# Sparse attention followed by a feed-forward block: band v of the first batch by one casting load, and the planner's figures anew

## The chip, the core and the metric

The kernel runs on one core of a Trainium2 chip. The metric is the device time in microseconds of one execution; the median of three runs of the kernel before is 298.2 us (298.0 to 298.53). Engines are named as in the profile: PE (matrix products and transposes), PEld (its weight loads), ACT, DVE, POOL and SP. POOL and SP also issue DMA transfers; only POOL's transfers convert fp32 to fp16 on the way in this kernel, and only SP issues transposing transfers. A step in which the text says "lands" is the moment at which a transfer's data is complete.

## What is computed

```python
# q, k, v: (8, 8, 576, 64) fp32; moe_w_in (512, 2048); moe_w_out (2048, 512); s, b: one number each
scores = scale * np.matmul(q, k.transpose(0, 1, 3, 2))
rel = pos[:, None] - pos[None, :]
mask_local = (rel >= 0) & (rel < 32)                                   # heads 0..3
mask_strided = (rel >= 0) & (pos[None, :] % 32 == pos[:, None] % 32)   # heads 4..7
attn = softmax(where(mask, scores, -1e9));  x = attn @ v               # then (4608, 512)
r = np.maximum(x @ w_in, 0.0)
out = (s * (r * r) + b) @ w_out
```

## The kernel before

**Attention.** There are eight batches of eight heads. Two heads make a pair, so a batch has four pairs: m = 0 and 1 are local (each query sees at most 32 keys back), m = 2 and 3 strided. A local pair works on 6 blocks of 96 queries against 128 keys (96 of the block and the 32 before it), a strided pair on 8 classes of 72 positions. `pair_steps` (from L474) writes a pair's work as a list of steps in fixed order: transposes of q and k on PE (L494, L502), their copies out of PSUM into `qD_*` and `kT*` (posted to ACT or DVE), score products (L623) into PSUM groups of 2 local or 3 strided products, one exponential per group on ACT (L641), AV products (L684) against `v_loc` or `v_str`, reciprocals and multiplications into `x_nat`, and transposes of `x_nat` (L731) whose copies give `xT`, the feed-forward input. Later batches do several of these transposes by SP's transposing transfers instead (`k_dma`, `q_dma`, `x_dma`, L546 to L599).

In batch 0 the mask is applied on PE: before each score product, a product of the identity with a tile of 0 and -30000 (`negs`) is written into the same columns (L620), and the score is added to it. In the other batches the exponentials are multiplied by 0 or 1 on DVE (L649).

**Band v.** For local heads `v_loc` holds v in blocks of 96 rows on partitions 32 to 127; partitions 0 to 31 hold the last 32 rows of the block before, which `rows_before` (L435) copies, once for each pair. A column of ones beside v gives the softmax's sums. For batch 0, SP loads heads 0 and 1 in fp32 into a corner of the still empty `w_out_sb` (`stage_v`, L309), POOL casts them (`cast_v`, L421) and copies the rows before. Heads 2 and 3 come by a casting transfer of POOL (L1365), which is issued behind q and k of all heads. Strided v is loaded to `vs` and cast from there to `v_str`.

**Feed-forward.** The tokens come in nine blocks T of 512. FF1 (`ff1`, L983) forms x @ w_in for 16 slices of 128, relu and square follow on ACT and DVE, FF2 (`ff2`, L1238) multiplies by w_out. From T = 2 on FF2, and for the last two blocks FF1 too, use a seven-product scheme of 2 x 2 blocks (`ff2_seven`, L951; `ff1_seven`, L1208). In the last block the last product, P3, is done for two halves t of 128 tokens, each of which is evicted on DVE and stored by itself (`store`, L878).

**Order.** Nothing loops on the chip: at build time a planner (`Plan`, L19) walks a modelled clock and writes one instruction order for each engine. Each PE step has keys that it needs, a cost in ns and keys that it makes; other engines' work is posted with the keys it waits for, a cost for each engine that may do it, and keys that it makes some latency later (`LAT`, L27). `flush` takes, among the posts that are ready, the one with the earliest ready time plus a weight of its kind (`ORDER`, L124). Times at which loads are expected are put in by hand: `AT` (L1371) for the first ones, `landing` (L1309), a ring on which each load adds its cost, for the rest. `due` (L1515) says how far attention should be ahead of the feed-forward steps. If no step is ready, `keep_running` (L1487) writes filler products on a spare PSUM bank (L1502), to keep PE running.

**Queues.** POOL's first transfers are q and k of the local heads, two heads at a time, then strided q and k, band v of heads 2 and 3, and strided v; then, gated by a one-element copy that reads the landed `qs` (L1386), the four quarters of w_in; then batch 1's loads with w_out. The fetches of batch b + 2 (`fetch_qk`, L1319) are held on POOL by one-element copies that read the strided kT transposes of batch b + 1 (L1323). In the plan such a fetch waits until `q` and `k` of batch b are used, by the keys in L1432 to L1437; for late batches the key `("q", ...)` is made by `q_spread` (L585), which spreads the transposed q over `qD` after the `qT` transfer has landed.

## Time and profile before

| | before |
|---|---|
| median of the runs | 298.2 us |
| profiled execution | 298.86 us |
| its span, first to last instruction | 297.1 us |
| PE busy | 290.5 us, 2802 products |
| DVE busy | 235.3 us |
| ACT busy | 194.3 us |
| POOL busy | 93.7 us |
| granted PE clock | 0.999 |
| FF1 products, L983 | 115.5 us |
| filler, L1502, to 20 us | 7.35 us |
| mask products, L620 | 28 |
| last product starts, ends | 293.30, 293.57 us |

The span is the stretch in which the profile sees instructions; the execution's own time is 1.8 us more than it. PE's products are pipelined, so their busy times overlap, and each lasts longer than the distance to the next: what a product costs when the stream is full is the distance between starts. The busy share is given over the whole span; the head, up to some 23 us, is limited otherwise than what follows, so that the windows by stage matter more than the sums.

### The profile page before, as it was taken

To read this page: it belongs to the slowest core of one execution; us is meant where nothing else is said; L and a number is where in the kernel's file an instruction comes from. 1 tells how busy PE (TensorE), PEld (TensorE's weight loads), DVE (VectorE), ACT (ScalarE), POOL (GpSimd) and SP (SyncE) were. 2 spreads that over 40 slices of the span, in tenths; PEclk is the share of its full clock that TensorE was granted. 3 is DMA by queue.
4 is the path that set the end of the run, shared out by engine and by line. 5 is a ranking of instruction groups with operands and counts; after the bars stand their busy time and mean duration, and the time that the engine had idled before them with its cause. 6 is when DMAs were issued, how large, how long until landed. Compare 5 with 4: busy or idle time off the path is not lost.

```text
span 297.1 us, 7092 instructions
## 1 busy us (share of the span) xinstructions
PE 290.5 (98%) x2802; PEld 220.0 (74%) x2802; DVE 235.3 (79%) x501; ACT 194.3 (65%) x336; POOL 93.7 (32%) x140
## 2 busy tenths in 40 slices
PE   8999999999999999999999999999999999999995
PEld 3775656666556568889767776768888989999984
DVE  5857888798966988787877896759898588888963
ACT  3577957898838798647774878469877545675400
POOL 8873624601980296009710394100000000000000
PEclk9999999999999999999999999999999999999999
DMA  8999999997999499989999999999230300110214
GB/s 136 189 206 203 218 180 184 223 171 119 109 195 149 67 132 138 170 173 122 148 136 144 182 170 105 143 140 207 44 97 0 108 29 9 71 38 3 95 48 142
DMA packets 106152, 38.19 MB, mean 129 GB/s; under 512 B 85414, under 2 KB 103974, under 8 KB 106118
## 3 DMA queue, kind: packets, MB, share of 16 engines
q0 software_dynamic: 60848, 18.23, 62.7%
q1 hardware_dynamic: 45270, 19.51, 36.0%
q8 instruction: 22, 0.36, 0.5%
q14 instruction: 12, 0.10, 0.1%
HBM read 36.99 MB, written 10.62 MB: 160 GB/s over the span
## 4 chain that ended last, share of the span: by engine, by line
PE 88%; DMA 6%; ACT 2%; DVE 2%; POOL 1%; issue 1%; ACTq 0%
PE ps_f L983 28%; PE ps_f L951 22%; PE ps_f L1238 8%; DMA v_loc<-in_v_dram 6%; PE ps_s L623 5%; PE ps_f L1208 3%; PE ps_a L684 3%; PE ps_s L1502 2%; PE ps_a L1208 2%; PE ps_s L951 2%; PE ps_t L1208 2%; PE ps_s L1208 2%; PE ps_t L951 1%; PE ps_s L1238 1%; PE ps_t L684 1%; PE ps_t L502 1%
## 5 line engine op out<-in xcount | busy, mean ns | idle before, releaser
L983 PE MATMUL ps_f<-xT,w_in_sb 128*128 128x512 f16 (+4 forms) x568 | 115.5, 331 | 0.3 <-ACT u L1009 0.3
L1009 ACT ACTIVATE u<-ps_f 128x512 f16<-128x512 f32 x104 | 61.0, 594 | 32.5 <-PE ps_f L983 31.8
L983 PEld LDWEIGHTS <-w_in_sb 128*128 128x128 f16 x576 | 57.4, 114 | 23.2 <-issue 0.5
L951 PEld LDWEIGHTS <-gT 128*128 128x128 f16 x608 | 58.4, 98 | 9.2
L951 PE MATMUL ps_f<-w_out_sb,gT 128*128 128x256 f16 x376 | 55.6, 273 | 0.0
L1017 ACT ACTIVATE gT<-u 128x1024 f16<-128x1024 f16 x29 | 30.7, 1057 | 0.8
L1238 PE MATMUL ps_f<-w_out_sb,gT 128*128 128x512 f16 x112 | 30.4, 379 | 0.0
L951 PE MATMUL ps_f<-w_mix,gT 128*128 128x256 f16 x176 | 25.1, 273 | 0.0
L641 ACT ACTIVATE p_str<-ps_s 72x432 f16<-72x432 f32 (+1 forms) x46 | 20.7, 482 | 6.4 <-PE ps_s L623 5.8
L711 DVE TENSOR_TENSOR x_nat<-ps_a,rec 96x384 f16<-96x384 f32 (+2 forms) x46 | 24.1, 523 | 0.6
L641 ACT ACTIVATE p_loc<-ps_s 128x384 f16<-128x384 f32 x46 | 21.4, 494 | 4.8 <-PE ps_s L623 4.3
L1019 DVE TENSOR_TENSOR gT<-u 128x1024 f16<-128x1024 f16 x27 | 18.5, 686 | 5.9 <-ACT u L1009 5.4
L819 DVE TENSOR_TENSOR gT<-gT 128x1024 f16<-128x1024 f16 x34 | 22.4, 678 | 0.6 <-ACT gT L1017 0.4
L382 POOL DMA_DIRECT2D v_loc<-in_v_dram x24 | 17.7, 757 | 8.6 <-DMA w_out_sb<-in_moe_w_out_dram 5.7
L951 PEld LDWEIGHTS <-S 128*128 128x128 f16 x176 | 17.1, 98 | 2.9
L1238 PEld LDWEIGHTS <-gT 128*128 128x128 f16 x128 | 11.4, 98 | 7.8
L387 POOL DMA_DIRECT2D v_str<-in_v_dram x16 | 13.0, 816 | 12.3 <-PE ps_f L983 3.6
L684 PEld LDWEIGHTS <-p_str 72*128 72x128 f16 x256 | 12.8, 98 | 5.1 <-ACT p_str L641 0.4
L1323 POOL COPY gate<-kT 1x1 f16<-1x1 f16 x6 | 1.5, 256 | 45.0 <-DMA kT<-ks 45.0
L951 PE MATMUL ps_f<-w_mix,S 128*128 128x256 f16 x112 | 15.5, 273 | 0.0
L701 DVE RECIPROCAL rec<-ps_a 96x6 f32<-96x6 f32 (+2 forms) x47 | 8.6, 182 | 8.6 <-PE ps_a L684 8.4
L1149 ACT ACTIVATE gT<-u 128x1024 f16<-128x1024 f16 x12 | 12.7, 1058 | 1.7 <-DVE u L1128 1.4
(237 smaller groups left out, 529.7 us busy)
## 6 DMA issues: line engine op xcount, KB each, us to landing
out_dram<-o SPq DMA_DIRECT2D x34, 256.0 KB, 2.9
w_in_sb<-in_moe_w_in_dram POOLq DMA_DIRECT2D x4, 512.0 KB, 9.7
w_out_sb<-in_moe_w_out_dram POOLq DMA_DIRECT2D x4, 512.0 KB, 9.9
qs<-in_q_dram POOLq DMA_DIRECT2D x6, 288.0 KB, 8.4
ks<-in_k_dram POOLq DMA_DIRECT2D x6, 288.0 KB, 9.7
v_loc<-in_v_dram POOLq DMA_DIRECT2D x24, 72.0 KB, 9.6
ql<-in_q_dram POOLq DMA_DIRECT2D x4, 288.0 KB, 9.0
kl<-in_k_dram POOLq DMA_DIRECT2D x16, 72.0 KB, 3.6
```

What stands on the lines that cost most here:

```text
L382: nc.gpsimd.dma_start(out=vl[LPAD:128, h, :, 0:D], in_=v_band(b, h))
L641: nc.scalar.activation(out=st["pw", g][0:nk, 0:2 * n * nq], in_=st["s", g][0:nk, 0:2 * n * nq], func=AF.Exp, scale=scale)
L684: nc.tensor.matmul(out=st["pa", g][:, n % 6, :], lhsT=st["pw", gp_][0:nk, i * nq:i * nq + WIDE], rhs=vt[0:nk, 2 * mm + e, j, :])
L711: nc.vector.tensor_tensor(out=x_at(0, cnt), in0=st["pa", g][0:nq, 0:cnt, 0:D], in1=st["rec", g][0:nq, 0:cnt].to_broadcast([nq, cnt, D]), o ...
L819: {"V": nc.vector, "P": nc.gpsimd}[eng].tensor_tensor(out=at(out), in0=at(x), in1=at(y), op=op)
L951: nc.tensor.matmul(out=gts[name, T, t][:, 0] if halves else gts[name, T][:, t], lhsT=lhs(k, t), rhs=rhs(k), start=fresh and k == 0 and (ha ...
L983: nc.tensor.matmul(out=gts["h", T, ft][:, lo:hi], lhsT=w_in_sb[ft // 4][:, ct].rearrange("p (x l) -> p l x", l=4)[:, ft % 4], rhs=xT[ct][: ...
L1009: nc.scalar.activation(out=u, in_=gts["h", T, ft], func=AF.Relu)
L1017: nc.scalar.activation(out=g, in_=u, func=AF.Square)
L1019: nc.vector.tensor_tensor(out=g, in0=u, in1=u, op=ALU.mult)
L1208: nc.tensor.matmul(out=st[bk][:, 256 * t:256 * t + 256], lhsT=lhs(t, c), rhs=rhs(c), start=fresh and t == c == 0, stop=t == c == 1, skip_g ...
L1238: nc.tensor.matmul(out=gts[id_], lhsT=gts[T][:, ft, ts * 128:(ts + 1) * 128], rhs=w_out_sb[:, ft, cols], start=(ft == 0), stop=(ft == NFT ...
```

## The change

Band v of batch 0 now comes for all four heads by the casting transfer that batch 1 already used (`load_vl`), issued behind the second pair of local keys and ahead of the strided q and k. The stage in `w_out_sb`, its memset, POOL's casts and the separate transfer of heads 2 and 3 are gone; the two row copies may each go to POOL or DVE. The memsets of `v_loc[0]` move ahead of those of `qD`.

The mask products of batch 0 are one for each PSUM group instead of one for each score product: the tile is broadcast over the 2 or 3 places, in a step of its own (`forbid`) ahead of the group's scores, which needs only the mask tile and a free bank.

The second half of the last P3 is done in two halves of 128 columns, each with its own eviction and store.

In the planner: the first landings (`AT`), the cost of later landings, and one more us on every pending load for each SP transfer (`shared`); shorter transfer latencies, by 3 us less where no load is pending; the fetch of a late batch waits in the plan for the `qT` transfer instead of `q_spread`; weights for single pairs of batch 0, an "ahead" for each sixth of the feed-forward's way, and new values for the weights. The last items set order alone and add no instruction.

```diff
-    LAT = {"A": 70.0, "V": 70.0, "P": 70.0, "D": 12000.0, "X": 7000.0, "Y": 12000.0}
+    LAT = {"A": 70.0, "V": 70.0, "P": 70.0, "D": 10000.0, "X": 7000.0, "Y": 10000.0}
...
+        self.ring, self.loads = 0.0, []
+
+    def landing(self, cost, keys, wait=700.0):
+
+        self.ring = max(self.ring, self.t + 2000.0) + cost
+        for k in keys:
+            self.done[k] = self.ring + wait
+        self.loads.append(keys)
+
+    def shared(self, cost=1000.0):
+
+        self.loads = [x for x in self.loads if self.done[x[0]] > self.t + 1000.0]
+        for x in self.loads:
+            for k in x:
+                self.done[k] += cost
+        if self.ring > self.t:
+            self.ring += cost
...
+    def late(self, k):
+
+        if not isinstance(k, tuple):
+            return 0.0
+        at = k[1] if len(k) > 1 and isinstance(k[1], tuple) else k[2:4] if k[0] == "in" else ()
+        if len(at) == 2 and at[0] == 0:
+            own = k[0] + (k[1] if k[0] == "in" else "") + "0" + str(at[1])
+            if own in self.LATER:
+                return self.LATER[own]
+        return 0.0 if k[2:3] == (0,) else self.LATER.get(k[0], 0.0)
...
+            if eng in "DXY":
+                self.shared()
...
-                self.done[k] = end + (6000.0 if soon else p[4] or self.LAT[eng])
+                self.done[k] = end + (6000.0 if soon else p[4] or self.LAT[eng] - (
+                    3000.0 if eng in "DY" and self.ring < self.t else 0.0))
...
+ORDER = {"g": 1500.0, "S": 1500.0, "in": 2500.0, "w_mix": -400.0, "wc": -400.0, "ev": -1500.0,
+         "c21": 2500.0, "c11": 1500.0, "c12": 2500.0, "C22": -1500.0, "fv": 500.0, "Vb": 1500.0,
+         "x": -800.0, "Ub": -800.0, "xc": 0.0, "fe": 500.0, "k": -1500.0, "fu": 1500.0,
+         "Va": -800.0, "p": 1500.0, "c22": 0.0, "Ua": 2500.0, "e": 500.0, "q": 1000.0, "r": 0.0,
+         "u": 0.0, "q01": 0.0, "p00": 1500.0, "x00": 2500.0, "invl01": -1500.0,
+         "invs00": -1500.0, "k01": 0.0, "r02": -400.0, "lead": 0.9, "r00": -800.0, "x01": 1000.0,
+         "invl00": 2500.0, "invs01": -1500.0, "ahead4": -0.05, "q02": -800.0, "ahead3": -0.1,
+         "r03": 1500.0, "q03": 500.0, "p02": 500.0, "k02": 1000.0, "r01": 500.0, "x03": -400.0,
+         "p01": 1000.0, "x02": 500.0, "q00": 500.0, "k03": -400.0, "p03": 1000.0, "ahead2": 0.05,
+         "ahead5": -0.1, "k00": -800.0, "ahead0": -0.05, "ahead1": 0.0, "SLACK": 400.0,
+         "ahead": 0.05}
...
-    vl_stage = w_out_sb.rearrange("p f m -> p (f m)").bitcast(FP32)[:, 0:NL // 2].rearrange(
-        "p (h t d) -> p h t d", h=2, d=D)
...
-    def stage_v(heads):
-        for h in heads:
-            nc.sync.dma_start(out=vl_stage[LPAD:128, h], in_=v_band(0, h))
-
     nc.sync.dma_start(out=ident, in_=h_ident.ap())
...
-    stage_v(range(2))
     nc.sync.dma_start(out=negs, in_=h_neg.ap())
     nc.vector.memset(ones16, 1.0)
+
+    def v_zero(i):
+        nc.vector.memset(v_loc[i][:, :, :, D:D + 1], 1.0)
+        nc.vector.memset(v_loc[i][0:LPAD, :, 0, :], 0.0)
+        nc.vector.memset(v_str[i][:, :, :, D:D + 1], 1.0)
+
+    v_zero(0)
     for i in range(2):
         nc.vector.memset(qD_loc[i], 0.0)
         nc.vector.memset(kT_loc[i][:, 0:LPAD], 0.0)
-    nc.vector.memset(vl_stage[0:LPAD], 0.0)
     for i in range(2):
         nc.vector.memset(qD_str[i], 0.0)
-    for i in range(NV):
-        nc.vector.memset(v_loc[i][:, :, :, D:D + 1], 1.0)
-        nc.vector.memset(v_loc[i][0:LPAD, :, 0, :], 0.0)
-        nc.vector.memset(v_str[i][:, :, :, D:D + 1], 1.0)
+    v_zero(1)
...
+        if b == 0:
+            load_vl(0)
...
-            src = vl_stage if loc else loaded[b, "vs"].rearrange(
-                "p (h t d) -> p h t d", h=4, d=D)
+            src = loaded[b, "vs"].rearrange("p (h t d) -> p h t d", h=4, d=D)
             for h in range(2 * mm, 2 * mm + 2):
-                copy_on(eng, out=dst[b % NV][0:np_, h, :, 0:D], in_=src[:, h])
-        n = nt * D
-        plan.post([key], {"P": 1000.0} if loc else {"P": 1160.0} if b == 0 else {"A": 2 * (170 + 0.83 * n), "V": 540.0}, g,
-                  [("cast", b, mm) if loc else ("in", "vs", b, mm)])
-        if loc:
-            rows_before(b, mm, ("cast", b, mm))
+                copy_on(eng, out=v_str[b % NV][:, h, :, 0:D], in_=src[:, h])
+        n = ST * D
+        plan.post([key], {"P": 1160.0} if b == 0 else {"A": 2 * (170 + 0.83 * n), "V": 540.0}, g,
+                  [("in", "vs", b, mm)])
 
     def rows_before(b, mm, key):
 
         hs = slice(2 * mm, 2 * mm + 2)
         vl = v_loc[b % NV]
-        src = vl_stage[:, :, :, 0:D] if b == 0 and mm == 0 else vl[:, :, :, 0:D]
 
         def g(eng):
-            copy_on(eng, out=vl[0:LPAD, hs, 1:LT, 0:D], in_=src[128 - LPAD:128, hs, 0:LT - 1])
-        plan.post([key], {"P": 800.0} if b == 0 and mm == 0 else {"P": 800.0, "V": 350.0} if b == 0 else {"A": 700.0, "V": 350.0}, g, [("in", "vl", b, mm)])
+            copy_on(eng, out=vl[0:LPAD, hs, 1:LT, 0:D], in_=vl[128 - LPAD:128, hs, 0:LT - 1, 0:D])
+        plan.post([key], {"P": 800.0, "V": 350.0} if b == 0 else {"A": 700.0, "V": 350.0}, g, [("in", "vl", b, mm)])
...
-                if i % per_s == 0:
+                if i % per_s == 0 and b >= PE_MASK:
                     st["s", g] = bank(group)
                 c = i % per_s * 2 * nq
-                if b < PE_MASK:
-
-                    nc.tensor.matmul(
-                        out=st["s", g][0:nk, c:c + 2 * nq], lhsT=ident[0:nk, 0:nk],
-                        rhs=neg_loc if loc else neg_str, start=True, stop=False)
                 nc.tensor.matmul(
                     out=st["s", g][0:nk, c:c + 2 * nq], lhsT=(st["k"][:, i * nq:i * nq + nk] if loc else st["k"][:, i, 0:SQ]),
-                    rhs=st["q"][:, i].rearrange("d e c -> d (e c)"), start=b >= PE_MASK, stop=True)
-
-            s = Step(f, (2 if b < PE_MASK else 1) * (2 * nq / 2.4 + 8), needs=[("q", id_), ("k", id_)],
-                     group=group if i % per_s == 0 else None)
+                    rhs=st["q"][:, i].rearrange("d e c -> d (e c)"), start=b >= PE_MASK, stop=True,
+                    skip_group_check=b < PE_MASK)
+
+            s = Step(f, 2 * nq / 2.4 + 8, needs=[("q", id_), ("k", id_)],
+                     group=group if i % per_s == 0 and b >= PE_MASK else None)
...
+        def forbid(i, group):
+
+            n = min(per_s, nt - i)
+
+            def f():
+                st["s", i // per_s] = bank(group)
+                nc.tensor.matmul(
+                    out=bank(group)[0:nk, 0:2 * n * nq], lhsT=ident[0:nk, 0:nk],
+                    rhs=(neg_loc if loc else neg_str)[:, None, :].to_broadcast([nk, n, 2 * nq]),
+                    start=True, stop=False, skip_group_check=True)
+            return Step(f, 2 * n * nq / 2.4 + 3, needs=[("negs",)], group=group)
+
         gr = None
         for i in range(nt):
             if i % per_s == 0:
                 gr = group_of("s", b, m)
+                if b < PE_MASK:
+                    steps.append(forbid(i, gr))
...
+        def store(i, k, of, plus, ts=slice(0, 2), ms=slice(0, 256)):
...
+            ends = [(t, k, slice(0, 256)) for t in range(2) for k in range(H)]
+            if last and key == "P3":
+                ends = ends[0:H] + [(1, k, slice(128 * c, 128 * c + 128)) for c in range(2)
+                                    for k in range(H)]
+            for t, k, ms in ends:
...
-                        s.keys = [("P3", T, t)]
-                        s.posts = [([("P3", T, t)], {"V": 420.0},
-                                    store(0, 1, "W", val("Ub"), slice(t, t + 1)),
-                                    [Ws[t]])]
+                        s.keys = [("P3", T, t, ms.stop)]
+                        s.posts = [([("P3", T, t, ms.stop)],
+                                    {"V": 480.0 if ms.stop - ms.start == 256 else 280.0},
+                                    store(0, 1, "W", val("Ub"), slice(t, t + 1), ms),
+                                    [Ws[t]] if ms.stop == 256 else [("P3", T)])]
...
-    def landing(cost):
-
-        nonlocal ring
-        ring = max(ring, plan.t + 2000.0) + cost
-
-        return ring + (6000.0 if plan.t > 60000.0 else 600.0)
...
-                arrive(both(name + "l", b), landing(4600))
+                plan.landing(2400, both(name + "l", b))
...
-            arrive(both(name, b), landing(2000 if b > 1 else 1200))
+            plan.landing(1600 if b > 1 else 1200, both(name, b))
...
-        plan.done["raw", "vl", b] = landing(4600)
+        plan.landing(2700, [("raw", "vl", b)])
...
-            arrive(both("vs", b), landing(5000))
+            plan.landing(3300, both("vs", b), 1200)
...
-    nc.gpsimd.dma_start(
-        out=v_loc[0].rearrange("p h t d -> p (h t) d")[LPAD:128, 2 * LT:4 * LT, 0:D],
-        in_=v.rearrange("b h (t p) d -> b p (h t) d", p=LQ)[0, :, 2 * LT:4 * LT])
     early_v(0)
-    plan.free["P"] = 7100.0
-    plan.free["V"] = 6500.0
-    AT = {"ql0": 5200.0, "kl0": 6900.0, "ql1": 7850.0, "kl1": 8700.0, "qs": 10200.0,
-          "ks": 12100.0, "vl0": 7100.0, "vl1": 13450.0, "vs": 15000.0}
+    plan.free["P"] = 8500.0
+    plan.free["V"] = 6000.0
+    AT = {"ql0": 4500.0, "kl0": 5500.0, "ql1": 6300.0, "kl1": 7100.0, "vl": 9400.0, "qs": 10400.0,
+          "ks": 12400.0, "vs": 14900.0}
...
+    plan.done["negs",] = 5000.0
...
-        ring = 13200.0
+        plan.ring = 13700.0
...
-    plan.done["raw", "v", True, 0] = AT["vl0"]
-    cast_v(0, True, 0, ("raw", "v", True, 0))
-    plan.done["raw", "vl", 0] = AT["vl1"]
-    rows_before(0, 1, ("raw", "vl", 0))
+            plan.landing(cost, [("w_in", c) for c in keys])
+
+    plan.done["raw", "vl", 0] = AT["vl"]
+    for mm in range(2):
+        rows_before(0, mm, ("raw", "vl", 0))
...
-                        [("q", (b, mk)) for mk in range(4)] + [("k", (b, mk)) for mk in range(4)] +
+                        [("qT" if b >= (QB_DMA if mk < 2 else QS_DMA) else "q", (b, mk))
+                         for mk in range(4)] + [("k", (b, mk)) for mk in range(4)] +
...
+        pos += order_.get(f"ahead{int(pos / 3)}", 0.0)
...
-        if len(order) == 2 and i1 % 4 == 0 and f1_pos[i1] > (f2[i2 - 1].pos if i2 else 0.0) + 1:
+        if len(order) == 2 and i1 % 4 == 0 and f1_pos[i1] > (f2[i2 - 1].pos if i2 else 0.0) + lead:
```

## The prediction

> **What bounds the kernel now.** I read the page first: busy shares and the slices.
>
> ```profile
> PE 290.5 (98%) x2802; PEld 220.0 (74%) x2802; DVE 235.3 (79%) x501; ACT 194.3 (65%) x336; POOL 93.7 (32%) x140
> ...
> PE   8999999999999999999999999999999999999995
> DMA  8999999997999499989999999999230300110214
> ```
>
> PE is busy throughout, but a busy PE also counts the filler products of L1502 that keep it running while nothing is ready. So next the windows of that line alone, stage by stage (span; PE busy and count; PEld; clock; DMA share; GB/s).
>
> ```profile
> 0.00:5.33 5.33, 4.28 (x10) 1.35 (x10) 1.00 0.64 115
> 5.33:10.00 4.67, 2.52 (x17) 1.23 (x16) 1.00 1.25 191
> 10.00:15.00 5.00, 0.33 (x3) 0.20 (x3) 1.00 1.46 186
> 15.00:20.00 5.00, 0.22 (x1) 0.10 (x1) 1.00 1.24 206
> 20.00:23.05 3.05, 0.00 (x0) 0.00 (x0) 1.00 1.24 208
> ```
>
> Filler ends at about 19 us; the rings run near 200 GB/s from 2.5 us on. Then the chain of waits inside this head (start, us, what):
>
> ```profile
> 1.05 4.34 PE ps_s L1502 x10
> ...
> 6.02 1.22 PE ps_s L1502 x8
> ...
> 7.62 0.70 PE ps_s L1502 x5
> ...
> 13.96 0.47 DVE kTs L404
> ...
> 18.01 0.82 ACT p_str L641 x2
> 18.84 0.82 ACT x_nat L707 x4
> ...
> 23.21 0.86 PE ps_f L983 x4
> ```
>
> Up to 8.7 us the chain is filler, that is, waiting for q and k to land; then copies on DVE and exponentials on ACT; from 23 us PE itself. From there PE's starts follow one another at the stream rate (in the whole chain of waits "23.21 3.67 PE ps_f L983 x17": 0.216 us each for 512 columns). The exceptions are in the late stage, in the timelines of ACT and PE:
>
> ```profile
> 195.39 0.73 ACT L404 COPY v_loc<-v_loc 32x640 f16<-32x640 f16 x1 [2.47 <-DMA v_loc<-in_v_dram]
> 196.66 1.02 PE L983 MATMUL ps_f<-xT,w_in_sb 128*128 128x512 f16 x4 [0.35 <-ACT u L1009]
> 200.61 0.32 PE L623 MATMUL ps_s<-qD_loc,kT_alt 128*128 128x192 f16 x2 [0.42 <-ACT p_loc L641]
> 293.61 0.48 DVE L882 SCALAR_TENSOR_TENSOR o<-ps_f,sb_all,Ub 128x256 f32<-128x256 f32 x1 [0.39 <-PE ps_f L951]
> ```
>
> ACT waits 2.47 us for the last batch's band v, and PE then loses 196.66 - (195.38 + 7 x 0.109) = 0.52 us and, at 200.61, 200.61 - (199.92 + 0.109) = 0.58 us. The last line is the last eviction; the span ends at 297.1, 3.0 us after it. PE's lost time is therefore: the head (start to steady stream, 23.05 us), about 1.5 us near 196, 200 and 239 us, and the tail of 3.5 us. All else is matmul columns, which the change leaves alone.
>
> **What the Trainium skill says.** "DMA: Bandwidth & Descriptors", Queues, rings and completion order: each DMA engine alternates by packets between the queues that have work. The trace agrees: SP's uncast v and POOL's q and k packets are mixed between 2.9 and 4.8 us. The same page, Specifications: runs below 512 B miss line rate. It agrees: batch 1's band v (the form that is now used for batch 0, 128 B written per run) landed 2.56 us after the load ahead of it (42.79, 45.35) for 288 KB, 115 GB/s where the head has 200. "TensorE: Matmul & The Clock Gate", Architectural detail: ACT and DVE run strictly in order; the u eviction held behind the v_loc copy above shows it.
>
> **The change, part by part.**
>
> *Band v.* Gone: two SP loads (144 KB each, fp32, 256 B runs), the 0.70 us DVE memset of the stage, and POOL's two casts and one row copy (8.39 to 10.2, 1.81 us). Added: one POOL issue of 1.22 us (row of batch 1's load) in place of one of 0.95, moved ahead of the qs, ks and vs issues, which start 1.2 us later; they land 5 us and more after issue, so the ring sets them, not the issue. By the ring: without SP's 288 KB (1.44 us at 200 GB/s) the four q/k loads land earlier, the first 4.89 -> about 4.3, the last 8.29 -> 6.9. Band v then takes 2.56: 9.5 us instead of 10.2 (pair 0 ready after the casts) and 13.2 plus 0.72 (pair 1). qs, ks and the half v took 13.22 - 8.29 = 4.93; with the other half (1.28) 6.2, so ks lands at about 13.1, 1.1 later than now (12.01), or 12.4 if the plan's new figure is right; vs about 14.5 (14.62 now). w_in chunk 0 stays at about 17.1: in front of it the ring carries only 144 KB less written. Its POOL gate waits for qs: 10.3 -> about 11.2, still 3 us before the ring would run dry.
>
> *What that does to the head.* Pair 1 (scores 11.26, AV 14.76, now) is done before ks lands, so ACT's p_loc exponentials (12.86 to 14.12) and DVE's qD_str and x_nat work no longer stand before the strided pairs. Now ks is transposed by 13.3 but its copy waits for DVE until 13.96, scores follow at 14.47. After: ks 13.1, transposes, copy of 0.46, scores at about 14.1. Six exponentials at 0.41 to 0.53 from 14.3 end near 17.2 instead of 18.84: 1.6 earlier. The v_str casts (four of 0.61 after vs) end at 17, so they do not undo it. PE: at 17.1, when w_in chunk 0 lands, about 1.1 us of attention is left (now: 1.8, and 0.7 of waiting), then 16 early FF1 products x 0.216 = 3.46 fill the chain of x_nat and xT: steady stream at 17.1 + 3.46 + 1.1 = 21.6 instead of 23.05. I take -1.5; ends: -2.5 (no attention left, earlier landing), +0.4 (ks 1.1 later and the copies behind it in today's order, less 0.7).
>
> *Wide masks.* 28 products become 12, same columns: 16 x 2.5 ns (82.5 against 80 for 192 columns) = 0.04 us. The first group of a pair, 0.165 or 0.19 us, can now run while q and k are being copied; the others stand between scores as before. Worth 0 to 0.7, and inside the -1.5, because PE has waits there anyway. A bank is held longer; two of four (s, f1) still turn.
>
> *Downstream cover.* Every load used after the head has over 3 us to spare: w_in chunk 1 lands 19.64, used 23.05; w_out chunks 2 and 3 land 39.82 and 42.79, used 42.88 and 46.23. Batch 1's band v lands 45.35, used 46.85, covered by 32 FF2 products (6.9 us). So the 1.5 us survives to 50 us.
>
> *Late gates, landings, order weights.* No instruction is added; order changes everywhere. POOL's late fetches are still held by the gate copies, which wait for the kT transposes of the batch before (16.3 us at 167.6), so an earlier place in the plan does not move them by itself. Cost from -1.5 (all late stalls gone) to +3 (below); I take 0.
>
> *Last output.* The last 8 products of 0.109 become 16 of 0.057: +0.04. The last eviction, 0.48 for 256 columns and 0.75 for 512, is by that slope 0.345 for 128: -0.135. The last store carries 64 instead of 128 KB in 512 B runs: 0 to -0.2, taken -0.1. Its issue (0.34) follows the other half's with 0.4 us between. Sum -0.2.
>
> Total: -1.5 - 0.2 = -1.7. The profiled execution took 298.86 with a span of 297.1, so span 295.4 and 297.2 for such an execution; against the median of 298.2: 296.5.
>
> **Rivals.**
>
> *Late landings too early in the plan (slower).* From a fetch the old plan expects band v after 2.0 + 4.6 + 4.6 + 2.0 + 2.0 + 4.6 + 6.0 = 25.8 us; the trace has 24.5 (batch 6: 133.94 to 158.44) and 26.2 (batch 7). The new one: 2.0 + 2.4 + 2.4 + 1.6 + 1.6 + 2.7 + 0.7 = 13.4 plus 1.0 per SP transfer; 7 and 10 lie in those windows: 20.4 and 23.4. So the row copy comes into ACT's or DVE's order 2.4 us earlier against its data for batch 7, 5.4 for batch 6. Today's 2.47 us of waiting costs PE 1.1; 4.9 would cost about 3.5, +2.4; 4.1 at batch 6 about 2.7. One of them: +2.4 to +3, so 298.2 - 1.7 + 3 = 299.5. It decides from about 1.5 us more of waiting behind such a copy. For it: the arithmetic. Against: for batch 5 the new figure, 17.4, is the trace's 17.8, the copy may go to DVE (half the price there), and the fetch's place in the plan also moves. Chance 0.28.
>
> *Given back.* PE comes 1.5 us earlier to a late stage whose loads do not move (DMA is at 9 tenths until slice 28, and the fetches wait for transposes): ACT's wait of 2.47 becomes 4. Only the tail is left: 298.0. For it: the DMA row. Against: SP's transposes wait for PE and DVE work, which moves too. Chance 0.10.
>
> *More.* The head as forecast and the new order takes the late waits away (1.1 at batch 7, 0.4 at 239): 295.0 to 295.4. Chance 0.18.
>
> *The forecast*, 295.8 to 297.3, has the remaining 0.44.
>
> **Numbers.** This kernel's runs lie within 0.2% of one another, so 0.2% (0.6 us) is what can be told from no change. Faster: forecast, more, and 0.02 of the given-back case: 0.64. Same: 0.08. Slower: 0.28. Low end: the better rival with a little over (294.8); high end: the slower rival with 0.3 over (299.8).
>
> **What would show it.** Right: the first transposes before 4.9 us; no CAST on POOL; AV of pair 1 before 12 us; first FF1 product near 17.3 and steady FF1 by 21.9; tail after the last product under 3.4 us. Wrong in the head: ks after 13.5 or filler between 10 and 17 above 1.5 us with steady FF1 at 23. Wrong late: a v_loc copy on ACT or DVE that waits over 4 us for its DMA near 150 to 200 us, with PE gaps after it, or new SP waits ahead of an xT transpose that FF1 needs. The forecast fails mostly if the late order decides instead of the head.

## The result and the profile after

The changed kernel takes 314.79 us (median of four runs, 313.42 to 317.21) against 298.19 (298.0 to 298.53): 1.056 times as long, 95% interval 1.0495 to 1.0633. The prediction was 296.5 with a range of 294.8 to 299.8. It was wrong in sign, and the measured time lies 15 us above the range. Single executions of a kernel are at times some us longer at a lower clock: the medians and ranges below contain them, the intervals of the ratio do not.

The page of the profiled execution (313.42 us, span 311.6), busy shares and slices:

```profile
PE 294.1 (94%) x2798; PEld 220.4 (71%) x2798; DVE 231.7 (74%) x499; ACT 195.4 (63%) x337; POOL 88.7 (28%) x136
...
PE   7899999999999799889799998899999999999992
...
PEclk9999999999999999999979999999999999999999
```

Before, PE's row was all nines between the first slice and the last. Now there are sevens and eights in the first two slices and between slices 14 and 26, that is from some 100 to 200 us, and the granted clock has one slice of 7 tenths.

The windows of the filler line in the head (span; PE busy and count; PEld; clock; DMA share; GB/s). The rings are the queues of the 16 DMA engines:

```profile
0.00:5.33 5.33, 3.70 (x9) 1.19 (x9) 1.00 0.60 85
5.33:10.00 4.67, 1.72 (x9) 0.77 (x10) 1.00 2.34 128
10.00:15.00 5.00, 1.40 (x11) 0.79 (x10) 1.00 1.29 181
15.00:20.00 5.00, 0.81 (x4) 0.39 (x4) 1.00 1.13 169
20.00:25.05 5.05, 0.49 (x2) 0.19 (x2) 1.00 1.24 208
```

From 10 us on there is 2.7 us of filler where there was 0.55, and between 5.33 and 10 us the rings moved 128 GB/s where they moved 191, although their packets are in flight for longer (2.34 against 1.25). Steady FF1 starts at 25.05 instead of 23.05.

The chain of waits (start, us, what), in the head and in the middle:

```profile
5.14 1.19 POOL qs L417 x2
6.33 0.59 POOL ks L417
6.92 8.29 DMA ks<-in_k_dram
25.22 4.53 PE ps_f L1038 x21
...
97.06 7.31 DMA kT<-ks
...
110.74 4.85 DMA kl<-in_k_dram
115.74 11.48 DMA kT_alt<-kl
128.69 7.01 DMA kT<-ks
```

Before, one load stood in this chain behind the head, the band v of the last batch:

```profile
178.55 16.76 DMA v_loc<-in_v_dram
```

The rest from 23 us on was nearly all PE. Now transposing transfers of SP, of 7 to 11 us each, set the pace, and the chain goes in a loop: kT lands at 104.37, only then does POOL's gate copy let the next batch's q and k be fetched, and kT_alt waits for that k. DMA's share of the chain is 23%; it was 6%. The transposing transfers themselves were not short before either: between 85 and 205 us a kT_alt took 8.4 us from issue to landing and an xT 10.4, but no step of the chain waited for them.

Where PE lost its time can be worked out from the starts: the distance to the next start, less what the columns cost in a full stream (0.216 us for 512, counted nothing for filler; a lower clock counts as loss). The columns themselves come to 281.2 us in both kernels.

| us lost by PE | 0 to 30 | 30 to 100 | 100 to 200 | 200 to the last product | after it | span |
|---|---|---|---|---|---|---|
| before | 8.9 | 0.7 | 1.2 | 0.4 | 3.51 | 297.1 |
| after | 10.8 | 0.5 | 11.6 | 2.1 | 4.24 | 311.6 |

So of 14.5 us, 10.4 are lost between 100 and 200 us, 1.9 in the head, and 2.4 at the end. The large gaps of the middle, in PE's timeline:

```profile
106.98 0.35 PE L781 MATMUL ps_t<-ident,x_nat 72*128 72x72 f16 x6 [1.86 <-DVE x_nat L761]
127.27 0.26 PE L658 MATMUL ps_s<-qD_loc,kT_alt 128*128 128x192 f16 x1 [1.02 <-DMA kT_alt<-kl]
135.74 0.57 PE L658 MATMUL ps_s<-qD_str,kT 128*72 128x144 f16 x6 [1.52 <-DMA kT<-ks]
156.02 1.25 PE L1038 MATMUL ps_f<-xT,w_in_sb 128*128 128x512 f16 x4 [2.22 <-ACT u L1064]
```

Two wait for a transposing transfer directly, the others for an instruction of DVE or ACT that itself waited for one (DVE's x_nat 2.9 us for xT). ACT's timeline just before the last one shows the link:

```profile
152.25 1.35 ACT L449 COPY qD_loc<-qTl 64x576 f16<-64x576 f16 x2 [2.70 <-DMA qTl<-ql]
154.00 1.35 ACT L449 COPY qD_loc<-qTl 64x576 f16<-64x576 f16 x2 [0.39 <-DMA qTl<-ql]
155.37 1.09 ACT L1064 ACTIVATE u<-ps_f 128x512 f16<-128x512 f32 x2
```

The copy stands in ACT's order ahead of the relu, and the relu's PSUM bank is what PE waits for. This gap costs more than its own length. In the windows around it (span; PE, PEld, DVE, ACT, POOL busy; clock; DMA share; GB/s) the granted clock is 0.58 for the next 4 us, about 1.7 us more:

```profile
150.00:156.00 6.00, 3.80 (x30) 2.63 (x29) 2.58 (x7) 3.31 (x6) 1.61 (x2) 1.00 2.10 123
156.00:160.00 4.00, 3.98 (x15) 2.08 (x15) 0.83 (x2) 1.68 (x4) 0.00 (x0) 0.58 1.48 182
160.00:164.00 4.00, 4.00 (x30) 2.83 (x29) 2.61 (x5) 3.33 (x8) 0.00 (x0) 0.99 1.82 116
```

Four products of 512 columns that start at 157.28 take until 158.99, 0.43 us each, twice the 0.216 of a full stream; half the clock was granted for 3.41 us, from 156.68 on.

What makes the transposing transfers late shows in the waits of SP's own queue between 85 and 205 us (us in total, times, longest), here those for q and k loads:

```profile
SPq L614 <- DMA ql<-in_q_dram: 14.1, 5, 6.6
...
SPq L595 <- DMA kl<-in_k_dram: 2.4, 4, 1.3
...
SPq L622 <- DMA qs<-in_q_dram: 1.7, 1, 1.7
```

The kernel before has one such line, of 1.4 us (for strided k). SP's timeline in the kernel before:

```profile
111.75 4.56 SPq L761 DMA_TRANSPOSE xT<-x_nat  x2
116.40 0.53 SPq L1253 DMA_DIRECT2D out_dram<-o  x1
117.04 2.67 SPq L574 DMA_TRANSPOSE qTl<-ql  x2
```

and in the changed one:

```profile
109.44 2.53 SPq L614 DMA_TRANSPOSE qTl<-ql  x2
113.47 3.75 SPq L595 DMA_TRANSPOSE kT_alt<-kl  x2
119.05 2.83 SPq L622 DMA_TRANSPOSE qT<-qs  x2
...
123.51 5.08 SPq L811 DMA_TRANSPOSE xT<-x_nat  x2
```

The next batch's q, k and strided q now stand ahead of xT, and SP, which issues in order, waits for their loads with xT behind it. In the longest of these waits, 6.6 us to 109.4, it issues nothing; xT's transfers are issued at 123.5 instead of 111.8. So far this is an observation; the runs below test it.

At the end, the timeline of DVE and PE:

```profile
305.57 0.75 DVE L932 SCALAR_TENSOR_TENSOR o<-ps_f,sb_all,Ua 128x512 f32<-128x512 f32 x1 [2.68 <-DMA out_dram<-o]
...
306.63 0.34 DVE L932 SCALAR_TENSOR_TENSOR o<-ps_f,sb_all,Ub 128x128 f32<-128x128 f32 x1
307.02 0.38 PE L1006 MATMUL ps_f<-w_out_sb,S 128*128 128x128 f16 x4 [1.64 <-DVE o L932]
308.72 0.35 DVE L932 SCALAR_TENSOR_TENSOR o<-ps_f,sb_all,Ub 128x128 f32<-128x128 f32 x1 [1.75 <-DMA out_dram<-o]
```

PE waits for the first quarter's eviction before it goes on with the second in the same PSUM tile, and that eviction is late because DVE has waited 2.68 us for a store two evictions earlier. The last eviction waits for a store again: three store buffers take turns.

### The profile page after: what moved, and what is told of

It is laid out like the page before. It is cut to its first block, busy times and chain, and to the rows that moved or that the text cites. A ratio compares the mean times of both kernels' runs of the same rounds, so it can differ in the third digit from the quotient of the medians.

```text
span 311.6 us, 7070 instructions
## 1 busy us (share of the span) xinstructions
PE 294.1 (94%) x2798; PEld 220.4 (71%) x2798; DVE 231.7 (74%) x499; ACT 195.4 (63%) x337; POOL 88.7 (28%) x136
## 4 chain that ended last, share of the span: by engine, by line
PE 66%; DMA 23%; POOL 3%; SPq 2%; DVE 2%; ACT 2%; issue 2%; DVEq 0%; POOLq 0%
PE ps_f L1038 20%; PE ps_f L1006 17%; DMA kT<-ks 7%; PE ps_f L1293 7%; PE ps_s L658 4%; DMA kT_alt<-kl 4%; DMA qT<-qs 3%; DMA qTl<-ql 3%; PE ps_f L1263 3%; DMA ks<-in_k_dram 3%; DMA out_dram<-o 2%; PE ps_a L1263 2%; PE ps_s L1263 2%; PE ps_s L1006 2%; PE ps_t L1263 2%; DMA kl<-in_k_dram 2%
## 5 line engine op out<-in xcount | busy, mean ns | idle before, releaser
L1038 PE MATMUL ps_f<-xT,w_in_sb 128*128 128x512 f16 (+4 forms) x568 | 118.1, 333 | 3.1 <-ACT u L1064 3.1
L1006 PE MATMUL ps_f<-w_out_sb,gT 128*128 128x256 f16 x376 | 54.2, 274 | 0.1
L1074 DVE TENSOR_TENSOR gT<-u 128x1024 f16<-128x1024 f16 x27 | 18.3, 680 | 15.7 <-ACT u L1064 15.5
L761 DVE TENSOR_TENSOR x_nat<-ps_a,rec 72x384 f16<-72x384 f32 (+2 forms) x46 | 23.9, 520 | 0.5
L677 ACT ACTIVATE p_loc<-ps_s 128x384 f16<-128x384 f32 x46 | 20.8, 491 | 4.9 <-PE ps_s L658 4.7
L1006 PEld LDWEIGHTS <-S 128*128 128x128 f16 x184 | 17.1, 98 | 4.1 <-issue 1.8
L734 PEld LDWEIGHTS <-p_str 72*128 72x128 f16 x256 | 13.5, 98 | 5.0
L432 POOL DMA_DIRECT2D v_str<-in_v_dram x16 | 13.0, 817 | 13.8 <-DVE rec L751 5.2
L751 DVE RECIPROCAL rec<-ps_a 72x6 f32<-72x6 f32 (+2 forms) x46 | 8.4, 182 | 9.1 <-PE ps_a L734 8.8
L869 DVE TENSOR_TENSOR S<-gT 128x1024 f16<-128x1024 f16 x18 | 12.2, 679 | 2.4 <-PE ps_f L1006 2.4
## 6 DMA issues: line engine op xcount, KB each, us to landing
v_loc<-in_v_dram POOLq DMA_DIRECT2D x24, 72.0 KB, 11.6
```

The lines of the kernel that those rows point to most:

```text
L677: nc.scalar.activation(out=st["pw", g][0:nk, 0:2 * n * nq], in_=st["s", g][0:nk, 0:2 * n * nq], func=AF.Exp, scale=scale)
L734: nc.tensor.matmul(out=st["pa", g][:, n % 6, :], lhsT=st["pw", gp_][0:nk, i * nq:i * nq + WIDE], rhs=vt[0:nk, 2 * mm + e, j, :])
L761: nc.vector.tensor_tensor(out=x_at(0, cnt), in0=st["pa", g][0:nq, 0:cnt, 0:D], in1=st["rec", g][0:nq, 0:cnt].to_broadcast([nq, cnt, D]), o ...
L869: {"V": nc.vector, "P": nc.gpsimd}[eng].tensor_tensor(out=at(out), in0=at(x), in1=at(y), op=op)
L1006: nc.tensor.matmul(out=dst[:, ms], lhsT=lhs(k, t), rhs=rhs(k)[:, ms], start=fresh and k == 0 and (halves or t == 0), stop=t == 1 and k == ...
L1038: nc.tensor.matmul(out=gts["h", T, ft][:, lo:hi], lhsT=w_in_sb[ft // 4][:, ct].rearrange("p (x l) -> p l x", l=4)[:, ft % 4], rhs=xT[ct][: ...
```

## The experiments

Each time is a median; "after" is 314.79, and the kernel before gave 298.12 to 298.43 beside them. The planner makes the order anew for each kernel, so most edits change the order too. The tables give the interval of the ratio to the kernel before.

### One part undone

`a_lat`: the old transposing latencies.

```diff
-    LAT = {"A": 70.0, "V": 70.0, "P": 70.0, "D": 10000.0, "X": 7000.0, "Y": 10000.0}
+    LAT = {"A": 70.0, "V": 70.0, "P": 70.0, "D": 12000.0, "X": 7000.0, "Y": 12000.0}
...
-                self.done[k] = end + (6000.0 if soon else p[4] or self.LAT[eng] - (
-                    3000.0 if eng in "DY" and self.ring < self.t else 0.0))
+                self.done[k] = end + (6000.0 if soon else p[4] or self.LAT[eng])
```

> The changed kernel with the old latencies of SP's transposing transfers in the plan (12 us, and no 3 us less when no load is pending). Theory L (the spreads of qT and qTl on DVE and ACT, and the products that read kT, are placed before those transfers land, because the plan now expects them 2 to 5 us earlier): the 10.7 us that DVE and ACT wait for qT and qTl and the 2.5 us that PE waits for kT go to under 2 us each, PE's loss between 100 and 200 us falls from about 10 us to under 3, time 305 to 307. Theory H (the head is 2 to 3.7 us behind the plan and everything that comes by DMA stays late): waits and time within 3 us of the changed kernel, 312 to 316. Theory W (the new weights and ahead values): the same as H.

`a_order`: the old weights (the whole `ORDER` of before, so neither single pairs' weights nor "lead").

```diff
-ORDER = {"g": 1500.0, "S": 1500.0, "in": 2500.0, "w_mix": -400.0, "wc": -400.0, "ev": -1500.0,
+ORDER = {"g": 1500.0, "S": 2500.0, "in": 2500.0, "w_mix": 0.0, "wc": 1000.0, "ev": 1000.0,
...
```

> The changed kernel with the old weights, ahead, slack and lead. Theory W (the new weights put spreads and copies in the wrong place): time 304 to 307, waits for qT and qTl under 2 us. Theories L and H: the order differs, but the waits for transposing transfers stay at 5 us or more in sum and the time stays at 311 to 317.

`a_band`: band v of batch 0 as before, with the old first landings.

```diff
-        if b == 0:
-            load_vl(0)
...
+    stage_v(range(2))
...
-    AT = {"ql0": 4500.0, "kl0": 5500.0, "ql1": 6300.0, "kl1": 7100.0, "vl": 9400.0, "qs": 10400.0,
+    AT = {"ql0": 5200.0, "kl0": 6900.0, "ql1": 7850.0, "kl1": 8700.0, "qs": 10200.0,
```

> The changed kernel with band v of the first batch loaded, cast and placed as before, with the old first landings; masks, last output and the rest of the planner stay new. All theories: ks of batch 0 lands near 12 us again and the steady stream starts 2 us earlier. Theory H: the loss between 100 and 200 us goes too, time 300 to 304. Theories L and W: only the head's 2 us come back, time 311 to 314.

`a_last`: the last product undivided.

```diff
-            if last and key == "P3":
+            if False:
                 ends = ends[0:H] + [(1, k, slice(128 * c, 128 * c + 128)) for c in range(2)
```

> The changed kernel with the last product undivided, as before. In the changed kernel PE waits 1.79 us between the two halves of the last product, because the second half writes the PSUM tile that the first half's eviction reads, and the last eviction waits 1.75 us for an output buffer. Expected: 2.0 to 2.7 us faster than the changed kernel, 312 to 313, tail after the last product back to 3.5 us; if instead only the output buffers hold the tail (three of them, and stores that take 3.9 us here), the gain is under 1 us.

| | us | range | ratio to before | PE lost 100 to 200 us |
|---|---|---|---|---|
| a_lat | 312.84 | 310.54 to 314.83 | 1.0402 to 1.0532 | 9.6 |
| a_order | 317.52 | 315.86 to 319.93 | 1.0600 to 1.0712 | 12.4 |
| a_band | 311.69 | 310.39 to 314.33 | 1.0404 to 1.0526 | 13.9 |
| a_last | 311.69 | 310.12 to 313.5 | 1.0409 to 1.0503 | 9.9 |

None of the four brings back more than about 3 us. The loss in the middle survives each: a_band repairs the head (PE lost 9.1 there), not the middle, so the middle does not follow from the late head alone; the weights are not the cause; the latencies alone are worth 2 us at most, less than the runs differ. What all four still share, besides the wide masks and the gate in the plan, is the landing figures. a_last gained a little more than expected, though the time after the last product, 4.17 us, did not go back to 3.5: undivided too, an eviction of 512 columns waits 2.13 us for a store there.

### One part alone

`b_plan` is the kernel before with the planner of the change (landings, latencies, gate, weights) and no new instruction; `b_band` has the casting load and its first landings alone, `b_masks` the wide masks alone with the order made anew, `b_last` the halved last output alone, whose order is otherwise that of before.

```diff
# b_plan
-    LAT = {"A": 70.0, "V": 70.0, "P": 70.0, "D": 12000.0, "X": 7000.0, "Y": 12000.0}
+    LAT = {"A": 70.0, "V": 70.0, "P": 70.0, "D": 10000.0, "X": 7000.0, "Y": 10000.0}
...
-            arrive(both(name, b), landing(2000 if b > 1 else 1200))
+            plan.landing(1600 if b > 1 else 1200, both(name, b))
...
# b_band
-    stage_v(range(2))
...
+        if b == 0:
+            load_vl(0)
...
# b_masks
+                if b < PE_MASK:
+                    steps.append(forbid(i, gr))
...
# b_last
+            if last and key == "P3":
+                ends = ends[0:H] + [(1, k, slice(128 * c, 128 * c + 128)) for c in range(2)
+                                    for k in range(H)]
```

> The kernel before with the new planner alone (landings, latencies, gate, weights); band v, masks and last output as before. Theory P (the new figures of the planner are what loses): waits of DVE and ACT for qT and qTl of 5 us or more, PE loses 5 us or more between 100 and 200 us, 304 to 310. Theory H (the later head shifts PE against the loads): 297 to 300, no such waits.

> The kernel before with the casting load of band v and its first landings alone; old planner figures, masks and last output. The head loses about 2 us more than before (ks near 15 us instead of 12). Theory P: that is all, 299.5 to 301.5. Theory H: PE loses 5 us or more between 100 and 200 us as well, 305 to 312. Theory R (any other order loses, because the old one happens to put every spread behind its transfer): a loss in the middle of 2 to 8 us, 302 to 310, as in the run with the wide masks alone.

> The kernel before with the wide mask products alone; the planner's figures, the loads and the last output are the old ones, but the order moves everywhere because the steps are others. Theory P and theory H: 297.3 to 299 (the masks are worth 0 to 0.7 us). Theory R: a loss in the middle of 2 to 8 us, 300 to 306.

> The kernel before with the halved last output alone; every other instruction stands where it stood. If the two halves of the product wait for one another through the shared PSUM tile and the last eviction for an output buffer, as in the changed kernel: 0.8 to 2.5 us slower, 299 to 300.7, with a PE gap of 1 us or more inside the last product. By the prediction's sum: 0.2 us faster, 298.0.

| | us | range | ratio to before | where PE lost more than before |
|---|---|---|---|---|
| b_plan | 305.31 | 304.46 to 306.56 | 1.0218 to 1.0283 | 100 to 200 us: 5.4 instead of 1.2 |
| b_band | 303.32 | 302.95 to 304.66 | 1.0148 to 1.0208 | head 11.0 instead of 8.9; 200 to 240 us 3.4 instead of 0.4 |
| b_masks | 304.4 | 301.1 to 308.6 | 1.0092 to 1.0246 | 100 to 200 us: 3.3; after the last product 5.26 instead of 3.51 |
| b_last | 299.87 | 299.54 to 300.2 | 1.0034 to 1.0073 | after the last product 4.44; 0.4 inside it |

Every part is slower by itself. b_band fits none of its expectations, being slower than the load alone was to make it, without the loss in the middle that the others name. In b_last PE's gap is 0.44 us, not 1. b_masks (1.7% by the ratio, some 5 us) shows what the prediction's rival described, in another kernel: in its ACT timeline the row copy of band v comes ahead of its load,

```profile
196.41 0.72 ACT L443 COPY v_loc<-v_loc 32x640 f16<-32x640 f16 x1 [4.29 <-DMA v_loc<-in_v_dram]
```

4.29 us of waiting, and PE loses 3.3 us between 150 and 200 us. But no new landing figure made this: the masks' steps alone reshuffled the order. To separate a part from its new order, the next runs held the order.

### The order held, and all the planner's times undone

`b_masks_same` writes the wide mask in the step of the first score product of its group, which leaves the order of DVE, ACT, POOL and SP as before; `b_band_same` puts the casting load into the old plan, with PE's and ACT's order as before; `j_slack` is the kernel before with one planner figure moved; `a_times` is the changed kernel with all the old times (landings of later loads, nothing per SP transfer, latencies, gate).

```diff
# b_masks_same
+                if b < PE_MASK and i % per_s == 0:
+                    nc.tensor.matmul(
+                        out=st["s", g][0:nk, 0:2 * n * nq], lhsT=ident[0:nk, 0:nk],
+                        rhs=(neg_loc if loc else neg_str)[:, None, :].to_broadcast([nk, n, 2 * nq]),
...
# b_band_same
-    stage_v(range(2))
...
+        if b == 0:
+            load_vl(0)
...
# a_times: the edits of a_lat and a_landing, and
-                        [("qT" if b >= (QB_DMA if mk < 2 else QS_DMA) else "q", (b, mk))
-                         for mk in range(4)] + [("k", (b, mk)) for mk in range(4)] +
+                        [("q", (b, mk)) for mk in range(4)] + [("k", (b, mk)) for mk in range(4)] +
...
# j_slack
-         "u": 0.0, "SLACK": 600.0, "ahead": 0.05}
+         "u": 0.0, "SLACK": 500.0, "ahead": 0.05}
```

> The kernel before with one wide mask product for each group, issued where the group's first narrow one stood: 28 become 12, and the order on DVE, ACT, POOL and SP stays exactly that of before. If the wide products themselves cost something: slower than 298.2 by over 0.6 us. If the 6 us of the run with the masks alone came from the order that moved with them (theory R): 297.9 to 298.4, no DMA waits beyond those of before.

> The kernel before with band v by one casting load behind the second local keys; casts and stage left out, but every post keeps its place and cost in the plan, so PE's and ACT's orders stay exactly those of before. Theory B (the load itself pushes the head back): ks near 15 us, the steady stream 2 us later, and the time 300 to 301; nothing lost between 60 and 190 us beyond before. Theory H (the later head also loses in the middle): 303 or more. If order alone made the loss of the run with the band alone: 298 to 299.

> The kernel before with nothing but the planner's slack changed from 600 to 500 ns, a value that has nothing to do with transfers; POOL's order stays, that of DVE, ACT and SP moves from some 30 us on. Theory R (the old order happens to fit the transfers, nearly any other loses some us in the middle): 300 to 306, DVE or ACT waiting for transfers for 2 us or more beyond before. Theory P (only the new figures lose): 297.6 to 299.

> The changed kernel with all old times in the plan (landings of later loads, latencies, gate); band v, masks, last output and weights new. Theory P in its narrow form (the new times lose): the waits for qT and qTl go under 2 us, 304 to 307. Theory R: no better than by chance, 307 to 316, with other waits in place of those.

| | us | range | ratio to before |
|---|---|---|---|
| b_masks_same | 299.59 | 298.29 to 303.16 | 1.0019 to 1.0053 |
| b_band_same | 303.19 | 302.39 to 304.11 | 1.0097 to 1.0192 |
| j_slack | 299.45 | 298.49 to 304.0 | 1.0017 to 1.0061 |
| a_times | 304.37 | 302.39 to 304.97 | 1.0127 to 1.0222 |

j_slack: this new order costs about 1 us, not 16. With b_masks above it was some 5 (1.2 of it with the masks alone, see below), with b_late7 below 2.4, so that a few us of any difference between two orders can come from the order alone.

b_band_same: with the order of PE and ACT held, the casting load still costs 4.8 us (5.1 in b_band), more than was expected of the load, and not in the middle: PE lost 0.2 between 100 and 200 us. Its windows show the same slow rings as the changed kernel: 89 GB/s to 5.33 us and 132 to 10 us, against 115 and 191. In its profiled execution the granted clock was also 0.82 between 10 and 15 us and 0.84 to 20 us, which is some 1.7 us; in those of b_band and of the changed kernel it stayed at 1.00 there. So what the late head costs is not one number.

b_masks_same: the masks in the old order are no gain. The time is 1.2 us longer, more than the 0.6 named ahead as the sign that the wide products cost something themselves, and here no order moved but PE's. The profiled execution (298.95) does not show a slower PE: the last product starts at 292.39 instead of 293.30. But DVE waits 2.00 us for a store at the end, and the last store is issued behind two others at 294.01 instead of 294.13, so that the span ends at 297.2 as before. What makes the median longer is open.

a_times takes 10.4 us off the changed kernel, and PE lost 0.1 between 100 and 200 us: the loss in the middle goes with the planner's times.

### Which time it is

`a_landing` brings back the old landing figures of later loads and nothing else. `a_wait_qk` and `a_wait_v` keep the changed kernel's ring and only put back the 6 us behind it, for q and k, or for v. `b_late7` is the kernel before, with band v of the last batch expected 3 us later.

```diff
# a_landing
-            self.done[k] = self.ring + wait
+            self.done[k] = self.ring + (6000.0 if self.t > 60000.0 else 600.0)
...
-            if eng in "DXY":
-                self.shared()
...
-                plan.landing(2400, both(name + "l", b))
+                plan.landing(4600, both(name + "l", b))
...
# a_wait_qk
-                plan.landing(2400, both(name + "l", b))
+                plan.landing(2400, both(name + "l", b), 6000.0)
...
# a_wait_v
-        plan.landing(2700, [("raw", "vl", b)])
+        plan.landing(2700, [("raw", "vl", b)], 6000.0 if plan.t > 60000.0 else 700.0)
...
# b_late7
-        plan.done["raw", "vl", b] = landing(4600)
+        plan.done["raw", "vl", b] = landing(4600) + (3000.0 if b == 7 else 0.0)
```

> The changed kernel with the old figures for later landings (4.6 us for a whole q, k or band v, 6 us more on every load after 60 us, nothing added for SP's transfers); the new transposing latencies stay. Theory S (the landing figures put SP's transposing transfers ahead of the loads that they read, and SP, which works in order, stands: 14.1 us for local q in the changed kernel, none in the kernel before): SP's waits for q and k loads are under 1 us together, the gaps of PE between 100 and 200 us fall from 11.6 to under 3 us, and the time is 303 to 307. Theory T (the latencies of the transposing transfers are the cause, and restoring them alone gave only 2 us because the landing figures hid it): 310 to 313, with copies that wait for qT, qTl and kT as before.

> The changed kernel, whose later q and k loads (local and strided) alone are expected 6 us after their place on the ring instead of 0.7; v is as changed. Theory S: SP's order is mended by this alone: 304 to 308, SP's waits for q and k loads under 2 us together. The rival of the prediction (the row copy of band v, planned too early, holds ACT or DVE): no gain, 311 to 316.

> The changed kernel, whose later v loads alone (band v and strided v) are expected 6 us after their place on the ring; q and k are as changed. Theory S: SP still waits over 8 us for local q, and the time stays at 311 to 316. The prediction's rival (the copy of band v): 306 to 310.

> The kernel before, with band v of the last batch alone expected 3 us later; all orders are as before up to some 190 us. If the 2.47 us for which ACT waits on that load costs PE the 1.1 us counted in the prediction: 297.0 to 297.4, with no wait of ACT for v_loc and a gap of PE under 0.3 us there. If the loss only moves to another step (as with every order tried so far): 298.0 to 299.5.

| | us | range | ratio to before | SP waits for q, k loads, 85 to 205 us | PE lost 100 to 200 us |
|---|---|---|---|---|---|
| after | 314.79 | 313.42 to 317.21 | 1.0495 to 1.0633 | 18.2 | 11.6 |
| a_landing | 302.96 | 301.92 to 303.48 | 1.0125 to 1.0189 | 0 | 0.2 |
| a_wait_qk | 307.57 | 305.12 to 309.92 | 1.0236 to 1.0321 | 0 | 0.0 |
| a_wait_v | 319.3 | 316.29 to 320.73 | 1.0636 to 1.0736 | 20.8 | 15.7 |
| b_late7 | 300.69 | 300.09 to 301.91 | 1.0053 to 1.0103 | 0 | 0.1 |

(a_wait_qk's profiled execution, 309.92 us, is the slowest of its four, at half the clock from 15.3 to 29 us; only its middle is read.) Theory S holds: the landing figures alone are worth 11.8 us, the 6 us for q and k alone 7.2, and the loss in the middle is gone with either. Both are more than any new order without these figures cost here (b_masks, some 5). That a_wait_qk stays 4.6 us behind a_landing was not followed up; its other executions had 0.983 to 0.991 of the clock, those of a_landing 0.992 to 0.998. The same 6 us for v alone made the kernel 4.5 us slower, outside both ranges expected; the loss in the middle grew with SP's waits, and why v's later place makes q's worse was not tried. Over all kernels the sign is plain: those with the new figures for q and k have 13.8 to 21.6 us of such waits of SP (a_lat, a_order, a_band, a_last, a_wait_v and b_plan too), those without 0 to 3.2. SP's timeline in a_landing has xT first again, with the loads landed when their turn comes:

```profile
112.34 4.66 SPq L809 DMA_TRANSPOSE xT<-x_nat  x2
117.56 0.33 SPq L1306 DMA_DIRECT2D out_dram<-o  x1
117.99 3.94 SPq L612 DMA_TRANSPOSE qTl<-ql  x2
```

Two things follow from the early figures: SP stands, and the copies of transposed q on ACT and DVE come too early in their own orders. Both go together in these runs, and no run moved one without the other, so that which of the two costs more stays open.

b_late7 did take away the 2.47 us for which ACT waited in the kernel before (PE lost 0.1 between 150 and 200 us, not 1.2), and the loss came back elsewhere, in PE's timeline at

```profile
231.83 0.49 PE L1208 MATMUL ps_s<-qD_loc,ks 128*128 128x256 f16 x3 [1.65 <-DVE qD_loc L1083]
```

so the kernel got 2.4 us slower, more than either expectation.

### The end, and what is left

`b_tail` is b_last, with the same instructions in the same order, but the last eviction writes to the free buffer of Va. `c_best` is the changed kernel without the three costly parts: the edits of a_band, a_landing and a_last together.

```diff
# b_tail
-                o = op.tile([128, 2, 256], FP32, tag="o", name="o")
+                o = (cp if ms.start else op).tile([128, 2, 256], FP32, tag="Va" if ms.start else "o", name="o")
```

> The kernel before with the halved last output, in the same order of instructions as in b_last (299.87), but the very last eviction writes to a buffer that is free (that of Va) instead of the fourth use of three store buffers. If the reuse of the store buffer is most of what the halved output costs, the last eviction no longer waits 1.59 us, the tail after the last product falls from 4.44 to 3.0 to 3.4 us, and the time is 298.2 to 298.7; PE's gap of 0.44 us between the two halves stays. If the gap or the smaller store is the cost: 299.5 and more.

> The changed kernel with three of its parts undone together: band v and its first landings, the landing figures of later loads, and the halved last output. What stays is the wide masks, the new transposing latencies, the gate in the plan and the new order weights. If the parts add up (a_landing 302.96, less 4.8 for the casting load and 1.4 to 1.6 for the last output): 296.5 to 297.5, which would be faster than before. If each new order has its own small losses, as the other variants of the kernel before show: 298.5 to 301.

b_last and b_tail, last eviction on DVE:

```profile
295.14 0.35 DVE L933 SCALAR_TENSOR_TENSOR o<-ps_f,sb_all,Ub 128x128 f32<-128x128 f32 x1 [1.59 <-DMA out_dram<-o]
```

```profile
294.24 0.35 DVE L933 SCALAR_TENSOR_TENSOR o<-ps_f,sb_all,Ub 128x128 f32<-128x128 f32 x1 [0.48 <-PE ps_f L1007]
```

b_tail took 298.92 us (298.29 to 302.31; ratio 0.9998 to 1.0036), with 3.38 us after the last product where b_last has 4.44. The store buffer was most of what the halved output cost in the kernel before; PE's gap of 0.44 us between the quarters stays in both, and the gain that the halves were counted at is not there even so.

c_best took 300.25 us (299.14 to 303.64; 1.0018 to 1.0064). The parts do not add up to a gain, as the second expectation had it: from a_landing to c_best there are 2.7 us, not the 6.2 to 6.4 counted, and in the profiled execution (302.46 us) PE lost 2.1 us between 150 and 200 us and 1.5 after that. No version that was run beats the kernel before. The 16.6 us go down in steps as 11.8 (landing figures) + 2.7 (casting load and halved output) + 1.8 (masks, latencies, gate and weights, with their order); the rest, 0.2 before rounding, is what the kernel before differed between the two sets of runs. Another order of undoing would give other steps: a_band and a_last, undone first, are 3.1 us each. The gate alone was not run.

## Why the prediction was wrong

**"Late gates, landings, order weights ... I take 0", from -1.5 to +3.** This is the step that failed: it measured +11.8 for the landings within the change, and +7.0 for the planner alone (b_plan). The arithmetic that should have warned was in the text, in the first rival: the new figures expect band v at 20.4 us and more where it lands at 24.5. But it was followed for one consumer only, the row copy on ACT. The same edit takes local q from 2.0 + 4.6 + 6.0 = 12.6 us after its fetch to 2.0 + 2.4 + 0.7 = 5.1; in the changed kernel the fetch that starts at 137.61 has its last local q at 144.07, 6.5 us, its last local k 10.9 (planned 7.5) and its strided k 15.1 (planned 10.7) later. (What `shared` adds for SP's transfers is left out of the planned times.) The old 12.6 was far too late, since in the kernel before the last local q lands 5.3 us after the start of its fetch at 133.94, and that was slack which the plan needed: q and k go to SP's transposing transfers, and a place too early in that queue holds everything behind it. The prediction asked what is queued behind a waiting instruction for ACT, and not for SP. The text named "new SP waits ahead of an xT transpose that FF1 needs" as what would prove it wrong late, and gave that no price.

**The rival, "late landings too early in the plan", 299.5.** The family was right, place and size were not: no copy of v_loc on ACT or DVE waits over 0.2 us between 85 and 205 us in the changed kernel. A gap can cost more than its length, too: after the one of 2.22 us the granted clock was 0.58 for 4 us, which is 4 x 0.42 = 1.7 us more. The Trainium skill, "TensorE: Matmul & The Clock Gate", What's actually happening, says that PE's clock falls to half after an idle window of about 3.4 us. The trace agrees on the rate (0.43 us for 512 columns); here a gap of 2.22 us came before it. The prediction priced gaps by their length alone.

**"I take -1.5" for the head.** Steady FF1 came 2.0 us later, not 1.5 earlier, and the load alone made the kernel before 4.8 us slower (b_band_same). Nearly every term was off. "the first 4.89 -> about 4.3, the last 8.29 -> 6.9": they landed at 4.85 and 8.31. SP's 288 KB had indeed taken time: without them POOL's queue had moved 0.33 MB by 5.33 us instead of 0.20, and the first local k landed at 5.63 instead of 6.70. But from 5 to 6.5 us it moved 0.15 MB where it moved 0.25 before, and the gain was gone. What slowed it there, before the first packet of band v, is open. "Band v then takes 2.56": it landed at 11.94, 3.63 after the last k. The 2.56 us were the distance between two landings at 42.79 and 45.35. The 2304 packets of that load start from 40.5 to 43.9 us, 3.5 us, partly beside the load ahead of it, so the term was mis-sized from a trace that showed it. Then strided k came at 15.2 instead of 13.1, the last strided v at 16.9 instead of 14.5, the gate of w_in at 13.41 instead of 11.2 and the first w_in at 19.12 instead of 17.1. The text had put the gate 3 us clear of a dry ring; at 13.41 that cover was gone, and the rings moved 65 GB/s between 15 and 16 us, where they had moved 206. The shape of the head was as forecast (pair 1 before strided work, no casts), only some 3.5 us later.

**"Worth 0 to 0.7", the wide masks.** Not seen: with the order held the last product came 0.9 us earlier in the profiled execution, but the time was 1.2 us above before, and why is open. What was missed is that the extra steps make the planner reorder everything (b_masks, some 5 us).

**"Last output, sum -0.2".** It measured +1.6 (b_last). The terms that were counted were right: the eviction takes 0.35 us (0.345 forecast). Two waits were not: the second quarter's products wait for the first one's eviction, 0.44 us, and the last eviction waits 1.59 us for a store buffer. The Trainium skill, "PSUM — Partial Sum Buffer", PSUM bank collisions raise a hardware error, says that the compiler's scheduler puts a dependency between instructions of different engines that touch one bank in the same 32 partitions, at whatever address. The 0.44 us fit that, since the quarters share no column; no run here shows that this rule made the wait. A look at who frees the buffer, three for what are now four stores in a row, would have shown the second.

**"Downstream cover ... survives to 50 us".** Right as to the cover: PE lost 0.5 us between 30 and 100 us in spite of w_in 2 us and band v of batch 1 3.7 us later. There was only no gain to carry.

## What to carry to other kernels

When a planner's expected times change, list every consumer of each changed key, engine by engine, the queue that issues transfers too, and compare each planned time with when the data lands in the trace; here the transposes placed too early in SP's queue cost what stood behind them. Later is not safe by itself: a_wait_v and b_late7 only moved an expected time later, and both got slower. When a transfer that competes is removed, follow the others to their last landing: here q and k gained until 5 us and had lost it again by 8.3. Take the size of a load from where its packets run, not from the distance of two landings. Splitting the last output brought nothing here even with a free store buffer, while its parts waited for one another in one PSUM tile.

## What was not expected of the hardware

Traffic behind the casting load of 288 KB in 128 B pieces was slower. Its packets took 31 ns each until 8.5 us and 69 to 176 ns after that; the strided q packets of 1024 B that followed took 195 to 300 ns between 8.5 and 10.5 us, where the kernel before had 98 to 112 ns. Over that stretch the packets of 1024 B took 139 to 213 ns on average in each of the ten kernels here with the load, and 98 to 102 in each of the ten without. In the kernel before, half as many of the same pieces, behind strided q and k, kept 31 ns. But the same load of 288 KB for batch 1 was there too, and did the same: its 2304 packets took 31 to 32 ns until 42 us and 71 on average after 42.5, the 768 B packets of the next load 142 ns beside them and 79 after 45 us, and the rings moved 128 GB/s between 42.5 and 43.5 us against 206 after 45.5. So it is not the size of the pieces alone, and it could have been read before the change; what else it takes was not tried.
